# Fillers ahead of the weight and token tiles, and one common back transpose for a pair of heads

## The chip, the cores and the metric

The kernel runs on one core of a Trainium2 chip. The metric is the device time of one execution in microseconds (us). A core has five engines with a queue each: TensorE (PE in the rows; PEld is its loading of weights), VectorE (DVE), ScalarE (ACT), GpSimd (POOL) and SyncE (SP). They wait for each other by semaphores.

## The reference

Three layers follow each other; all numbers are float32, B = 4, S = 576, 8 heads of 64, model width 512.

```python
# 1 attention over the last row's maximum less tau
scores = q @ k.T / 8 ; scores = where(scores >= max - tau, scores, -1e9)
attn = exp(scores - max) ; attn /= sum(attn) + 1e-9 ; x = attn @ v
# 2 mixing along the sequence, then a feed-forward layer (512 -> 2048 -> 512)
u = x + (x.transpose(0, 2, 1) @ U @ V).transpose(0, 2, 1)
y = u + maximum(u @ w_ch1, 0) @ w_ch2
# 3 a causal gate of five taps, and two projections
gate = sigmoid(sum_k conv_w[k] * y shifted by 4 - k)
out = (gate * (y @ w_val)) @ w_out
```

The seven weights come as float64 and are turned into float32 by bit operations on the chip.

## The kernel before, in words

**Memory.** A tile takes a number of bytes in each of the 128 partitions of the on-chip memory (SBUF), and starts are rounded up to 32 bytes. Pools grow from the left end, or, with `side="right"`, from the right end. As the built program lays them out, every large tile on the left starts 96 bytes past a multiple of 256: `u`, `ring`, `w1_0`, `w2_0`, the staging tiles `raw`, `wt`, `wf`, the attention tiles `u4`, `vst`, `t_st`, `pt`, `pk`, `os`, `vt`, `vk`, `ns`, `e`, and later `y` and `w1_1`. Every tile on the right starts 224 bytes past one: `ld` (`qn`, `kn`, `tn`), `qk`, `st`, `bd`, and later `us`, `h` (and `g` in its place) and `w2_1`. The identity `idn` starts at 128. Steps inside the weight and token tiles are multiples of 512 bytes.

**Attention** (`attention`, from line 223) goes through 16 pairs of heads (`p`), each with 9 row tiles (`i`); one step of this is a slot `s = 9 p + i`. In a slot the code first issues the short work of the other engines and then PE's. `soft_max` (VectorE: negated scores and their minimum) comes first; then four phases 0 to 3 of functions put off by `later(slot, phase, fn, name)`, sorted within a phase by `LATE_ORDER`; `soft_exp` (ScalarE) follows phase 1 and `soft_mask` of the slot before (VectorE: mask and row sum) phase 2. Then PE gets the next slot's scores and the events that `put` gave this slot, sorted by `ORDER`: `prep_T` transposes q and k of the next pair (`tm`), `trans_main` and `trans_tail` transpose the masked exponentials (`xm`, `xk`; ScalarE copies them to `pt`, `pk`), `pv` multiplies by v (`o`, copied to `os`), `back` turns the result round again (`b`), and `mix_t`, `mix_u`, `mix_ut` add the mixing along the sequence (`t`, `u`, `ut`). All of these use one pool of four PSUM tiles. The order on every engine is this order of the code.

A pair's nine row tiles form three groups: group 0 is the 64 tail rows of both heads, groups 1 and 2 are 256 rows each. `pv` of groups 0 and 1 stands at slot offset 8, that of group 2 at 12; `back` of groups 0 and 1 at 10, that of group 2 at 14; `mix_t` at 15. Counted modulo 9, these are slots 8, 3, 1, 5 and 6. Each `back` takes one PSUM tile; in the slot after it VectorE multiplies by the reciprocal sums `r` into `ring` (L521), and for group 0 ScalarE does (`rb` L534, `ring` L536, twice). The first `back`'s VectorE and ScalarE instructions read the same PSUM tile, and VectorE's waits for ScalarE's. `soft_mask` makes the reciprocals in two parts, after row tiles 4 and 8 (L441, L442).

**Dense part.** `h1` multiplies 512 (last block 256) tokens of `us` by a chunk of `w_ch1` (`a`), `ch` multiplies `h` by a chunk of `w_ch2` (`c`): four chunks, five token blocks, taken alternately. `passes` (L771) does each in three products of high and low parts; a block is 4 x 12 = 48 matmuls. The weights of chunk c are in `w1_0`/`w2_0` for even c and in `w1_1`/`w2_1` for odd c. `val` (`v`, with `w1_0`) and `proj` (`p`, weights `g`, moving `w2_0`, L917) end the kernel; `val` waits for the gates, which VectorE sums up (L855). `dense_back` lays out `y` and `w1_1` where attention's tiles were.

Of the kernel before, what the change touches and what calls it, by code (L numbers as in the profile page):

```python
# [21 lines left out]
F32 = mybir.dt.float32  # L22
F32R = mybir.dt.float32r
I32 = mybir.dt.int32
U32 = mybir.dt.uint32
ACTF = mybir.ActivationFunctionType
ALU = mybir.AluOpType
# [9 lines left out]
def attention_moe_kernel(  # L37
# [15 lines left out]
    nc = tc.nc  # L53
    B, H, S, D = q.shape
# [8 lines left out]
    KD = DM // 128  # L63
    FC = 512
    NCH = DFF // FC
    SM = 512
    TL = S - SM
# [11 lines left out]
    const = ctx.enter_context(tc.tile_pool(name="const", bufs=1))  # L79
    idn = const.tile([128, 128], F32, name="idn")  # L80
# [4 lines left out]
    cw = const.tile([128, KC, KD], F32, name="cw")  # L85
    u = const.tile([128, KD, T], F32, name="u")
    ring = const.tile([128, 1280], F32, name="ring")
    w1_0 = const.tile([128, 2, KD, FC], F32R, name="w1_0")
    w2_0 = const.tile([128, 2, KD, FC], F32R, name="w2_0")
    wst_p = ctx.enter_context(tc.tile_pool(name="wst", bufs=2))  # L90
# [83 lines left out]
    class Staged:  # L174
# [20 lines left out]
    AT = {  # L195
        "pv": (8, 12), "t": 15, "ut": 18, "u": 18, "Tq": 0, "Tk": 1, "Tt": 2, "stA": 4, "bd": 4, "stB": 5,
        "lq": 1, "lv": 5,
    }
# [22 lines left out]
    low, top, mid, front, ps_x, ps_s, extra = (scope() for _ in range(7))  # L221

    def attention(dense_front, dense_mid, dense_back):
        setup = low.enter_context(tc.tile_pool(name="setup", bufs=1))
        sm_p = low.enter_context(tc.tile_pool(name="sm", bufs=4))
# [23 lines left out]
        st8 = [dict() for _ in range(NP)]  # L249

        def xtile(name):
            return x_ps.tile([128, 512], F32, tag="x", name=name)
# [47 lines left out]
        def later(s, k, fn, name=""):  # L300
            late[k].setdefault(s, []).append((LATE_ORDER.get(name, 0), fn))
# [126 lines left out]
        def row(p, i):  # L428
            return st8[p]["e", i][:, 1 - i % 2 if i else 0, :]

        def soft_mask(p, i):
            d = st8[p]
            e = row(p, i)
            nc.vector.scalar_tensor_tensor(  # L434
                out=e, in0=d.pop(("ns", i)), scalar=d.pop(("th", i))[:, 0:1], in1=e, op0=ALU.is_le, op1=ALU.mult,
                accum_out=d["sum"][:, i:i + 1],
            )
            if i in (4, 8):
                n = slice(0, 5) if i == 4 else slice(5, 9)
                t = d["sum"][:, n]  # L440
                nc.vector.tensor_scalar(out=t, in0=t, scalar1=1e-9, scalar2=None, op0=ALU.add)  # L441
                nc.vector.reciprocal(out=d["r"][:, n], in_=t)  # L442


        def trans_main(s, p, i):
# [41 lines left out]
        def pv(s, p, *gs):  # L487
            d = st8[p]
            ops = []
            for g in gs:  # L490
                n = 256 if g else TL
                pt = d.pop(("pt", g))
                o = xtile("o")
                nc.tensor.matmul(  # L494
                    o[:, 0:n], vk[p % 2].rearrange("p h d -> p (h d)"), d.pop(("pk", g)), start=True, stop=False
                )
                for j in range(4):
                    for hh in range(2):
                        rhs = pt[:, hh, j, :] if g else pt[:, j, hh * TL:(hh + 1) * TL]
                        ops.append((o[hh * D:(hh + 1) * D, 0:n], vt[p % 2][:, hh, j, :], rhs, j == 3))  # L500
                d["os", g] = os = o_p.tile([128, n], F32, tag=f"os{n}", name="os")
                later(s + 1, 0, lambda os=os, o=o, n=n: nc.scalar.activation(
                    out=os, in_=o[:, 0:n], func=ACTF.Copy), "o")
            for o, lhs, rhs, stop in ops:
                nc.tensor.matmul(o, lhs, rhs, start=False, stop=stop)  # L505


        def back(s, p, *gs):
            x = xtile("b")
            for g in gs:  # L510
                back_group(s, p, g, x)

        def back_group(s, p, g, x):
            d = st8[p]
            os, r = d.pop(("os", g)), d["r"]
            if g:
                for m in range(2):
                    nc.tensor.transpose(x[:, m * 128:(m + 1) * 128], os[:, m * 128:(m + 1) * 128], idn)

                def dve():  # L520
                    nc.vector.tensor_tensor(  # L521
                        out=x_of(p)[:, 2 * g - 2:2 * g, :].rearrange("p t (h d) -> p (t h) d", h=2),
                        in0=x[:, 0:256].rearrange("p (t d) -> p t d", t=4),
                        in1=r[:, 4 * g - 3:4 * g + 1].unsqueeze(2).to_broadcast([128, 4, D]), op=ALU.mult,
                    )

                later(s + 1, 2, dve, "n")
            else:
                x = x[0:TL, 256:384]
                nc.tensor.transpose(x, os[:, 0:TL], idn)  # L530
                rb = sm_p.tile([TL, 1], F32, tag="rb", name="rb")

                def act():
                    nc.scalar.activation(out=rb, in_=r[TL:128, 0:1], func=ACTF.Copy)  # L534
                    for hh, sc in ((0, r[0:TL, 0:1]), (1, rb)):
                        nc.scalar.activation(  # L536
                            out=x_of(p)[0:TL, 4, hh * D:(hh + 1) * D], in_=x[:, hh * D:(hh + 1) * D],
                            func=ACTF.Copy, scale=sc,
                        )

                later(s + 1, 1, act, "nt")

        def x_of(p):
            return ring[:, p % 2 * 640:(p % 2 + 1) * 640].rearrange("p (t d) -> p t d", t=5)
# [39 lines left out]
        for m in range(2):  # L584
# [7 lines left out]
            out=rv[0][:, 0:8 * R].rearrange("p (t r) -> p t r", t=4),  # L592
            in_=moe_U[0:SM, :].rearrange("(t p) r -> p t r", p=128),
# [3 lines left out]
        def load_V(a, o, c, n):  # L597
# [5 lines left out]
            out=qscale, in0=tau_sb, scalar1=0.0, scalar2=float(D) ** -0.5, op0=ALU.is_ge, op1=ALU.mult  # L603
# [39 lines left out]
        def put(s, what, *a):  # L643
            slots[s].append((what, a))

        for p in range(NP):
            s0 = 9 * p
            for i in range(9):
                put(s0 + i + 2, trans_main, p, i)
                if i % 2 == 0:  # L650
                    put(s0 + i + 2, trans_tail, p, i)
            put(s0 + AT["pv"][0], pv, p, 0, 1)
            put(s0 + AT["pv"][0] + 2, back, p, 0, 1)
            put(s0 + AT["pv"][1], pv, p, 2)
            put(s0 + AT["pv"][1] + 2, back, p, 2)
            if p + 1 < NP:
                s1 = s0
                put(s1 + AT["Tq"], prep_T, p + 1, "q")
                put(s1 + AT["Tk"], prep_T, p + 1, "k")
                put(s1 + AT["Tt"], prep_T, p + 1, "tail")  # L660
                put(s1 + AT["stA"], stacks, p + 1, 0)
                put(s1 + AT["bd"], tails, p + 1)
                put(s1 + AT["stB"], stacks, p + 1, 1)
            put(s0 + AT["t"], mix_t, p)
            put(s0 + AT["ut"] - (p == NP - 1), mix_ut, p)
            put(s0 + AT["u"] - (p == NP - 1), mix_u, p)
# [7 lines left out]
        for s in range(NS):  # L674
            p, i = divmod(s, 9)
# [12 lines left out]
            for m in (0, 1, 2, 3):  # L688
                for _, fn in sorted(late[m].pop(s, []), key=lambda x: x[0]):
                    fn()  # L690
                if m == 1 and live:
                    soft_exp(p, i)
                if m == 2 and 1 <= s <= 9 * NP:
                    soft_mask(*divmod(s - 1, 9))
                wtick(m)
# [21 lines left out]
        for _ in dense_front:  # L717
            work.tick()
        dense_back()
        ps_x.close()  # L720

# [3 lines left out]
    w1, w2 = [[w1_0], []], [[w2_0], []]  # L725
# [84 lines left out]
    def dense_back():  # L810
        extra.close()
        low.close()
        big = ctx.enter_context(tc.tile_pool(name="big", bufs=1))
        p1["y"] = big.tile([128, KD, B, YP], F32, name="y")
        w1[1].append(big.tile([128, 2, KD, FC], F32R, name="w1_1"))
        w2_p = ctx.enter_context(tc.tile_pool(name="w2", bufs=1, side="right"))
        w2[1].append(w2_p.tile([128, 2, KD, FC], F32R, name="w2_1"))
        nc.gpsimd.memset(p1["y"][:, :, :, 0:KC - 1], 0.0)
# [146 lines left out]
    with tc.manual_schedule():  # L965
        attention(dense_front(), dense_mid, dense_back)
        dense()
# [30 lines left out]
```

## Time and profile before

| | us |
|---|---|
| three runs | 869.0, 868.8, 867.21 (median 868.8) |
| profiled execution, its own time | 867.01 |
| its span, first to last instruction | 865.1 |
| PE busy | 834.6 (96%) |
| VectorE busy | 615.9 (71%) |
| ScalarE busy | 439.9 (51%) |
| GpSimd busy | 233.4 (27%) |

The share of busy time is a mean over stretches that differ, so the profile is read by stretch. A row of the chain of waits gives start, length and what PE or another engine did there; `x48` is the number of instructions joined in it. [...]

### The profile page before, as it was taken

How to read it: one execution, taken by the hardware profiler on the slowest of the kernel's cores; microseconds unless marked ns; L12 is line 12 of the kernel's file. 1: busy time of each engine (PE TensorE's matmuls, PEld its weight loads, DVE VectorE, ACT ScalarE, POOL GpSimd, SP SyncE). 2: the span in 40 equal slices, each digit the busy share in tenths (PEclk: the TensorE clock that was granted, in tenths of full speed). 3: DMA queues.
4: the chain of work that ended last, by engine and by line, in shares of the span. 5: the costliest groups of instructions: out<-in, count | busy, mean ns of one | idle time of the engine just before them, and what ended most of it. 6: DMA issues, size and time to landing. Idle time of an engine off the chain costs nothing.

```text
span 865.1 us, 14250 instructions
## 1 busy us (share of the span) xinstructions
PE 834.6 (96%) x5084; PEld 692.8 (80%) x5084; DVE 615.9 (71%) x1341; ACT 439.9 (51%) x890; POOL 233.4 (27%) x342
## 2 busy tenths in 40 slices
PE   8899999999999999899999999999999999999998
PEld 7687787788787887678888888888888888878886
DVE  5589889889989987436784685357753588988850
ACT  4487888888887887422333333133321334344532
POOL 6645422533322422001331243003420133200000
PEclk9799999999999999999999999999999999999999
DMA  5676755666676651001220122002110111001111
GB/s 129 147 151 124 172 125 125 153 154 137 151 168 135 132 113 44 0 1 49 73 74 25 48 74 74 1 1 84 62 50 1 41 57 49 1 1 49 49 49 74
DMA packets 63423, 68.07 MB, mean 79 GB/s; under 512 B 43333, under 2 KB 46549, under 8 KB 63354
## 3 DMA queue, kind: packets, MB, share of 16 engines
q1 hardware_dynamic: 61786, 64.07, 30.3%
q0 software_dynamic: 1424, 3.10, 1.3%
q8 instruction: 41, 0.67, 0.3%
q14 instruction: 28, 0.23, 0.1%
q10 hardware_dynamic: 144, 0.00, 0.0%
HBM read 35.89 MB, written 4.72 MB: 47 GB/s over the span
## 4 chain that ended last, share of the span: by engine, by line
PE 77%; DVE 9%; ACT 8%; issue 2%; SPq 1%; POOL 1%; DMA 1%; ACTq 0%; DVEq 0%; POOLq 0%
PE a L771 23%; PE c L771 20%; PE o L505 7%; PE s L395 6%; PE p L917 6%; PE xm L451 5%; PE v L771 5%; DVE u L855 3%; ACT e L423 2%; PE t L551 2%; PE o L494 2%; ACT pt L460 2%; DVE ns L409 1%; DVE e L434 1%; ACT qk L310 1%
## 5 line engine op out<-in xcount | busy, mean ns | idle before, releaser
L771 PE MATMUL a<-us,w 128*128 128x512 f32 (+1 forms) x960 | 205.6, 373 | 0.0
L771 PE MATMUL c<-h,w 128*128 128x512 f32 (+1 forms) x960 | 203.0, 370 | 1.3 <-ACT u L573 1.3
L771 PEld LDWEIGHTS a<-us,w 128*128 128x128 f32 x960 | 167.6, 188 | 33.9 <-issue 0.4
L771 PEld LDWEIGHTS c<-h,w 128*128 128x128 f32 x960 | 167.4, 188 | 33.7 <-ACT u L573 1.7
L779 ACT ACTIVATE h<-a 128x512 fp32r<-128x512 f32 (+1 forms) x80 | 44.2, 554 | 202.9 <-PE a L771 202.9
L780 DVE SCALAR_TENSOR_TENSOR h<-a,h 128x512 fp32r<-128x512 f32 (+1 forms) x80 | 51.0, 637 | 112.3 <-ACT h L779 112.2
L423 ACT ACTIVATE e<-ns,nm 128x576 f32<-128x576 f32 x144 | 111.5, 774 | 36.1 <-DVE ns L409 32.7
L128 POOL TENSOR_TENSOR wf<-wf,wt 128x512 f32<-128x512 f32 (+2 forms) x43 | 57.1, 1329 | 262.7 <-DVE wt L123 262.7
L424 POOL TENSOR_TENSOR th<-nm,tau_eff 128x1 f32<-128x1 f32 x144 | 72.8, 506 | 195.5 <-DVE ns L409 193.9
L434 DVE SCALAR_TENSOR_TENSOR e<-ns,th,e 128x576 f32<-128x576 f32 x144 | 119.8, 832 | 5.9 <-POOL th L424 5.5
L409 DVE TENSOR_SCALAR_CACHE_REDUCE ns<-s 128x576 f32<-128x576 f32 x144 | 107.8, 748 | 19.8 <-PE s L395 19.3
L451 PE MATMUL xm<-idn,e 128*128 128x128 f32 x576 | 88.5, 277 | 9.4 <-DVE e L434 5.1
L395 PE MATMUL s<-st 128*128 128x288 f32 x480 | 94.0, 317 | 1.3 <-DVE ns L409 1.1
L460 ACT ACTIVATE pt<-xm 128x512 f32<-128x512 f32 x144 | 84.5, 587 | 2.7 <-PE xm L451 0.6
L451 PEld LDWEIGHTS xm<-idn,e 128*128 128x128 f32 x576 | 69.1, 141 | 15.3 <-ACT pt L460 8.7
L395 PEld LDWEIGHTS s<-st 128*128 128x128 f32 x480 | 68.7, 191 | 13.5 <-DVE ns L409 6.6
L505 PE MATMUL o<-pt,vt 128*64 128x256 f32 (+1 forms) x768 | 70.9, 335 | 0.0
L505 PEld LDWEIGHTS o<-pt,vt 128*64 128x64 f32 x768 | 42.1, 140 | 25.2 <-issue 10.8
L169 POOL TENSOR_TENSOR w<-wf,w 128x512 fp32r<-128x512 f32 x36 | 54.2, 1518 | 10.3 <-ACT w L167 10.3
L832 DVE TENSOR_TENSOR y<-c,y 128x64 f32<-128x64 f32 (+4 forms) x96 | 39.9, 449 | 22.0 <-PE c L771 22.0
L855 DVE SCALAR_TENSOR_TENSOR u<-y,cw,u 128x576 f32<-128x576 f32 x64 | 55.0, 872 | 0.6
L756 DVE TENSOR_TENSOR us<-u,us 128x1024 fp32r<-128x1024 f32 (+1 forms) x40 | 46.8, 1211 | 9.2 <-ACT us L755 9.1
(108 smaller groups left out, 1043.8 us busy)
## 6 DMA issues: line engine op xcount, KB each, us to landing
raw<-in_moe_w_ch_dram SPq DMA_DIRECT2D x32, 512.0 KB, 4.1
st<-qk SPq DMA_DIRECT2D x30, 256.0 KB, 4.1
st<-qk SPq DMA_DIRECT2D x15, 432.0 KB, 4.0
st<-qk SPq DMA_DIRECT2D x45, 144.0 KB, 4.5
out_dram<-ring SPq DMA_DIRECT2D x18, 256.0 KB, 2.0
st<-qk SPq DMA_DIRECT2D x15, 288.0 KB, 4.9
qn<-in_q_dram SPq DMA_DIRECT2D x28, 128.0 KB, 3.8
kn<-in_k_dram SPq DMA_DIRECT2D x28, 128.0 KB, 3.6
```

The lines of the kernel that those rows point to most:

```text
L128: nc.gpsimd.tensor_tensor(out=dst, in0=dst, in1=tf, op=ALU.add)
L169: lo_eng.tensor_tensor(out=lo, in0=w, in1=f(hi), op=ALU.subtract)
L395: nc.tensor.matmul(s[:, n, 0:HS], lhs, rhs[:, n * HS:(n + 1) * HS], start=(m == 0), stop=(m == len(ops) - 1))
L409: nc.vector.tensor_scalar(out=ns.rearrange("p (a b) -> p a b", a=2), in0=s, scalar1=-1.0, scalar2=3.0e38, op0=ALU.mult, op1=ALU.min, accum ...
L423: nc.scalar.activation(out=row(p, i), in_=d["ns", i], func=ACTF.Exp, bias=nm[:, 0:1], scale=-1.0)
L424: nc.gpsimd.tensor_tensor(out=th, in0=nm, in1=tau_eff, op=ALU.add)
L434: nc.vector.scalar_tensor_tensor(out=e, in0=d.pop(("ns", i)), scalar=d.pop(("th", i))[:, 0:1], in1=e, op0=ALU.is_le, op1=ALU.mult, accum_o ...
L451: nc.tensor.transpose(x[:, j * 128:(j + 1) * 128], e[:, c + j * 128:c + (j + 1) * 128], idn)
L460: later(s + 1, 0, lambda: nc.scalar.activation(out=dst, in_=x.rearrange("p (j c) -> p j c", j=4), func=ACTF.Copy), "x")
L505: nc.tensor.matmul(o, lhs, rhs, start=False, stop=stop)
L771: nc.tensor.matmul(ps[:, 0:m1], lhs, rhs, start=(m == 0), stop=(m == len(ops) - 1))
L855: nc.vector.scalar_tensor_tensor(out=g, in0=y[:, e, b, k:k + S], scalar=cw[:, k, e:e + 1], in1=g, op0=ALU.mult, op1=ALU.add)
```

## The change

Two tiles that nothing uses are laid out: `pad_low`, 160 bytes, on the left behind `ring`, and `pad_top`, 224 bytes, as the first on the right. All tiles behind them move by as much, to starts that are multiples of 256; `u`, `ring` and `idn` stay. `w1_1` is laid out ahead of `y`, not behind it. `back` is called once a pair, at slot offset 14, for all three groups: the tail rows get a PSUM tile of their own (`x0`), groups 1 and 2 share one, and one VectorE instruction multiplies both. ScalarE's tail rows follow in phase 0 of the slot behind. The reciprocals are made in one part, after row tile 8. The copy of `o` to `os` is put off to phase 1 where it was phase 0.

```diff
+    const.tile([128, 40], F32, name="pad_low")
+    ctx.enter_context(tc.tile_pool(name="pad", bufs=1, side="right")).tile([128, 56], F32, name="pad_top")
     w1_0 = const.tile([128, 2, KD, FC], F32R, name="w1_0")
...
-            if i in (4, 8):
-                n = slice(0, 5) if i == 4 else slice(5, 9)
-                t = d["sum"][:, n]
+            if i == 8:
+                t = d["sum"]
                 nc.vector.tensor_scalar(out=t, in0=t, scalar1=1e-9, scalar2=None, op0=ALU.add)
-                nc.vector.reciprocal(out=d["r"][:, n], in_=t)
+                nc.vector.reciprocal(out=d["r"], in_=t)
...
-                later(s + 1, 0, lambda os=os, o=o, n=n: nc.scalar.activation(
+                later(s + 1, 1, lambda os=os, o=o, n=n: nc.scalar.activation(
...
+        def back(s, p):
             d = st8[p]
+            r = d["r"]
+            x0, x = xtile("b0"), xtile("b")
+            for g in (0, 1, 2):
+                os = d.pop(("os", g))
+                if not g:
+                    nc.tensor.transpose(x0[0:TL, 0:128], os[:, 0:TL], idn)
+                    continue
+                for m in range(2 * g - 2, 2 * g):
+                    nc.tensor.transpose(x[:, m * 128:(m + 1) * 128], os[:, m % 2 * 128:(m % 2 + 1) * 128], idn)
+            rb = sm_p.tile([TL, 1], F32, tag="rb", name="rb")
+
+            def act():
+                nc.scalar.activation(out=rb, in_=r[TL:128, 0:1], func=ACTF.Copy)
+                for hh, sc in ((0, r[0:TL, 0:1]), (1, rb)):
+                    nc.scalar.activation(
+                        out=x_of(p)[0:TL, 4, hh * D:(hh + 1) * D], in_=x0[0:TL, hh * D:(hh + 1) * D],
+                        func=ACTF.Copy, scale=sc,
+                    )
+            later(s + 1, 0, act, "nt")
+            later(s + 1, 2, lambda: nc.vector.tensor_tensor(
+                out=x_of(p)[:, 0:4, :].rearrange("p t (h d) -> p (t h) d", h=2),
+                in0=x.rearrange("p (t d) -> p t d", t=8),
+                in1=r[:, 1:9].unsqueeze(2).to_broadcast([128, 8, D]), op=ALU.mult,
+            ), "n")
...
             put(s0 + AT["pv"][0], pv, p, 0, 1)
-            put(s0 + AT["pv"][0] + 2, back, p, 0, 1)
             put(s0 + AT["pv"][1], pv, p, 2)
-            put(s0 + AT["pv"][1] + 2, back, p, 2)
+            put(s0 + AT["pv"][1] + 2, back, p)
...
+        w1[1].append(big.tile([128, 2, KD, FC], F32R, name="w1_1"))
         p1["y"] = big.tile([128, KD, B, YP], F32, name="y")
-        w1[1].append(big.tile([128, 2, KD, FC], F32R, name="w1_1"))
```

## Rows read from the trace of the kernel before

**Rows 1.** Stretch, us, busy us (count) of PE, PEld, DVE, ACT, POOL, PEclk, DMA
```profile
100.00:345.00 245.00, 233.89 (x1965) 195.15 (x1962) 213.09 (x594) 198.61 (x456) 82.89 (x164) 1.00 0.61 135
345.00:725.00 380.00, 375.95 (x1789) 311.03 (x1788) 227.31 (x385) 118.08 (x192) 86.50 (x62) 1.00 0.14 44
725.00:771.50 46.50, 44.81 (x241) 38.44 (x239) 43.09 (x70) 19.56 (x32) 6.62 (x4) 1.00 0.00 1
771.50:865.10 93.60, 89.63 (x407) 73.15 (x407) 55.59 (x84) 35.98 (x62) 0.00 (x0) 1.00 0.14 51
```

**Rows 2.** Chain of waits, dense part: start us, length us, what
```profile
563.15 5.74 PE c L771 x48
...
580.05 11.15 PE c L771 x48
591.20 11.15 PE a L771 x48
...
680.75 10.89 PE c L771 x48
691.64 11.16 PE a L771 x48
```

**Rows 3.** Chain of waits, from the end of the gates on
```profile
770.08 1.42 DVE us L756 x3
...
805.09 11.20 PE p L917 x48
```

**Rows 4.** Groups of instructions by form, 512-column matmuls: count | busy us, mean ns
```profile
L771 PE MATMUL a<-us,w 128*128 128x512 f32 x768 | 182.0, 395 | 0.0
L771 PE MATMUL c<-h,w 128*128 128x512 f32 x768 | 179.5, 392 | 1.3 <-ACT u L573 1.3
...
L917 PE MATMUL p<-w,g 128*128 128x512 f32 x216 | 50.9, 395 | 0.0
L771 PE MATMUL v<-us,w 128*128 128x512 f32 x192 | 45.7, 396 | 1.7 <-DVE us L756 1.1 <-ACT us L755 0.6
```

**Rows 5.** Chain of waits through one pair of the attention stage
```profile
167.29 0.20 ACT rb L534
...
167.51 0.51 ACT ring L536 x2
...
169.17 0.49 ACT pt L460
...
169.70 0.66 PE xm L451 x4
...
174.91 0.22 PE b L518 x2
...
176.21 1.13 PE t L551 x10
```

**Rows 6.** Chain of waits: the first and the last `rb` on it
```profile
43.94 0.20 ACT rb L534
...
329.95 0.20 ACT rb L534
```

**Rows 7.** Instructions in order of time, VectorE's multiplication in that pair
```profile
168.06 0.42 DVE L521 TENSOR_TENSOR ring<-b,r 128x256 f32<-128x256 f32 x1 [1.17 <-ACT ring L536]
```

**Rows 8.** Groups of instructions by form, VectorE: count | busy us, mean ns | idle before
```profile
L521 DVE TENSOR_TENSOR ring<-b,r 128x256 f32<-128x256 f32 x32 | 13.5, 421 | 7.9 <-ACT ring L536 7.8
...
L320 DVE TENSOR_TENSOR qk<-tm,qk 128x512 fp32r<-128x512 f32 x16 | 11.0, 685 | 0.0
...
L442 DVE RECIPROCAL r<-sum 128x5 f32<-128x5 f32 x16 | 3.0, 190 | 0.6
```

**Rows 9.** Chain of waits, the mix of the next pair
```profile
196.66 1.35 PE t L551 x10
```

**Rows 10.** Instructions in order of time, ScalarE ahead of that mix
```profile
195.99 0.59 ACT L460 ACTIVATE pt<-xm 128x512 f32<-128x512 f32 x1
```

**Rows 11.** Who waited for whom, GpSimd, 340 to 380 us: in total, times, longest
```profile
POOL y L818 <- PE ut L572: 31.9, 1, 31.9
```

More of the change, by code (lines that the diff above doesn't have):

```diff
@@ L505, in pv @@
                 nc.tensor.matmul(o, lhs, rhs, start=False, stop=stop)
[L508 to L513, printed above, removed]
-            d = st8[p]
[L515 to L524, printed above, removed]
-                    )
[L527 to L541, printed above, removed]
```

## The prediction

> **What bounds the kernel now.** I read the busy times by stretch first [rows 1], then the chain of waits inside each stretch [rows 2, 3, 5, 6 and 9], then single lines and their waits. [...] From 725 to 771.5 us VectorE is busy 43.09 of 46.5 us: the gates bind. In the attention stretch (100 to 345 us) PE is busy 234 of 245 us, with VectorE at 213 and ScalarE at 199: three engines near their limit, and the chain changes between them.
>
> **Part 1, the fillers.** They add no instruction. What they change is where a tile starts. Before, every large tile on the left of the memory starts 96 bytes past a multiple of 256 and every one on the right 224 bytes past one; after, those behind the fillers start at 0. So between a left and a right tile the distance is 128 modulo 256 before, and 0 after; between two tiles on one side it stays 0.
>
> The trace holds both cases. The blocks of 48 matmuls of 512 columns are alike in everything but their tiles. For `c` in chunks 1 and 3, moving `h` and weights `w2_1` are both on the right: a block takes 10.89 us (680.75 in [rows 2]). For `c` in chunk 2 the weights are `w2_0`, on the left: 11.15 us (580.05). `a` always has `us` on the right and `w1` on the left: 11.15 and 11.16 us. `p` has `g` on the right as weights and `w2_0` on the left as moving tile: 11.20 us [rows 3]. So I read the equal residue of the two tiles that PE reads together as worth 11.155 - 10.89 = 0.265 us a block, 5.5 ns a matmul. All five shown run at the same granted clock, and `c` and `a` alternate, so the load on the other engines does not sort them.
>
> The counts [rows 4], in blocks of 48: `a` 768/48 = 16, `c` 16, of which 8 (chunks 0 and 2) are slow, `v` 4, `p` 4.5. All of `a`, the slow `c` and `p` lie where the chain is PE. The first `v` block waits behind the gates (VectorE's 1.42 us of `us` ends before it [rows 3]), so what it gains is lost; 3 count. 16 + 8 + 3 + 4.5 = 31.5 blocks x 0.265 = **8.3 us less**. Blocks of 256 columns take 5.74 us with equal residues (563.15 in [rows 2], chunk 1); I take no change for them. Bounds of this term: nothing (the residue is not the cause), and on the other side that start addresses at 0 help more than equal residues do. From 256 to 512 columns a block grows by 10.89 - 5.74 = 5.15 us, so 512 columns cost 10.30 us a block by columns alone; 31.5 x (11.155 - 10.30) + 8 x (10.89 - 10.30) = 31.6 us less is the far end. I take 8.3 because it is the one that rows show, with no new kind of address.
>
> [...]
>
> In the attention stage operands mostly shift together and keep their distances. The identity, which lies ahead of the filler, does not; its distance to the transposed tiles changes from 32 or 160 to 128 (mod 256). Transposes take 0.11 us each (two in 0.22 us, [rows 5]); bounds: nothing, or the 5.5 ns above on each of 960 (60 a pair by the code), 5.3 us more. I take nothing: a transpose has a quarter of those columns.
>
> `w1_1` and `y` change places. `y` is a whole number of 256 bytes long, so this is not needed for the residue. The clearing of `y` now waits 31.9 us for the last mix of attention [rows 11]; that wait moves to earlier readers, and `w1_1`, whose writes come only after, takes over the wait for the mix. Cost 0, hidden by the dense blocks.
>
> **Part 2, the common back.** Per pair it removes one VectorE add and one reciprocal (0.19 us each by the reciprocal's row, so 0.38), and joins two multiplications of 256 elements (0.421 us each) to one of 512 (0.685 us by a VectorE row of that width) [rows 8]. It moves three transposes from slot 1 of the nine to slot 5, and the three ScalarE instructions of the tail rows (`rb`, `ring` twice) from slot 2 to slot 6.
>
> *What goes.* In 12 of 16 pairs these ScalarE instructions are on the chain: [rows 6] has the first and last. They run from 167.29 to 168.02 [rows 5], 0.73 us, and behind them come `qk`, `e`, and the `pt` copy (169.17) for which PE's next transposes wait until 169.70. Taken from there, `xm` starts 0.73 us earlier: 12 x 0.73 = 8.8 us less. VectorE's multiplication also waits there, 1.17 us, for ScalarE to finish with the same PSUM tile [rows 7]; with two tiles (`x0`, `x`) that wait goes, but it is off the chain in those pairs. What is late next is still ScalarE's row of copies and exponentials, so the whole 0.73 counts.
>
> *What comes back.* Slot 5 is on PE's path: `b`, two transposes, is on the chain at 174.91 [rows 5]. Three more at 0.11 us are 0.33 us; x 15 = 5.0 us more. In slot 6 the mix `t` now needs the whole product and the tail rows at once. In [rows 5] `t` takes 1.13 us, unhindered; in every second pair, where weight conversion delays ScalarE, 1.35 us [rows 9]. There the `pt` copy ends at 195.99 + 0.59 = 196.58 [rows 10]; the moved 0.73 us follow it, so `t` can start at 197.31 where it started at 196.66: 0.65 us, of which 0.33 is counted. 7 pairs x 0.32 = 2.2 us more. The longer multiplication ends 0.685 - 0.421 = 0.26 us later but starts 0.38 us earlier, since the add and reciprocal ahead of it are gone; in the 3 pairs where VectorE is the chain this gives 3 x 0.12 = 0.4 us less. Bounds per pair: nothing comes back, or all of it does, 0.33 + 0.73 + 0.26 = 1.32 us. Moving the `os` copy from phase 0 to 1 costs nothing: no other ScalarE work lies between.
>
> Attention: -8.8 + 5.0 + 2.2 - 0.4 = **2.0 us less**.
>
> **Sum.** 8.3 + 2.0 = 10.3 us off the profiled execution's 867.0: 856.7. The median of the runs shown is 1.8 us above that execution; I put half of this on top and predict 857.5.
>
> **Rivals.** *1. The fillers do nothing.* [...] Against: 10.89 us (once 10.93) in the six 512-column `c` blocks of chunks 1 and 3 that the chain shows, of which 680.75 is the fifth, and 11.1 to 11.2 elsewhere. Time: 867.0 - 2.0 + 0.9 = 866.
>
> *2. Starts at 0 free the rest too.* For: by column cost alone a block would take 10.30 us; 0.59 us remain even in the fast blocks, whose tiles start at 224. Against: nothing in the trace has such a start. Time: 867.0 - 31.6 - 2.0 + 0.9 = 834. [...]
>
> *3. The back costs nothing in slots 5 and 6*, because PE there catches up with VectorE anyway. For: VectorE is 87% busy in the stretch. Against: `b` and `t` are on the chain. Time: 867.0 - 8.3 - 9.2 + 0.9 = 850.
>
> *4. Slower: slot 6 becomes the stop.* `t` waits for the ScalarE rows, for the long multiplication and for the added transposes one after the other: 1.32 us x 15 = 19.8, less 8.8, is 11.0 us more; with the fillers' 8.3, 867.0 + 2.7 + 0.9 = 870.5. It decides from (8.8 + 8.3)/15 = 1.14 us a pair on. For: `t` already waits in every second pair. Against: ScalarE has its idle time in the slots just behind, and the tail rows are needed only by the last fifth of `t`, if its PSUM tile is free.
>
> **Chances.** Forecast 0.60, its own range 853 to 861; rival 1 0.15, rival 2 0.07, rival 3 0.10, rival 4 0.08. The range 847 to 866 holds the forecast, rival 3 and most of rival 1. Within 0.2% (1.7 us, about what can be told from no change) lies part of rival 1: same 0.06. Slower: rival 4 and a little, 0.09. Faster 0.85.
>
> **What would show it.** Right: `a`, `p` and all `c` blocks at 10.9 us; no ScalarE `rb` and `ring` between `pk` and `qk` on the chain; `t` at 1.1 to 1.4 us; VectorE's multiplication without its wait for ScalarE. Wrong: `a` blocks still at 11.15 (rival 1) or near 10.3 (rival 2); transposes above 0.11 us; `t` beyond 1.8 us in most pairs (rival 4).

## The result

The changed kernel takes 856.91 us (median of four runs, 854.32 to 859.88) against 868.15 us of the kernel before beside it: a ratio of 0.9879, 95% interval 0.9851 to 0.9907. Two later sets, beside other runs of the kernel before, gave 0.9874 (0.9857 to 0.9892) and 0.9873 (0.9849 to 0.9898). The prediction was 857.5. The profiled execution is one of the quickest: 854.32 us, span 852.4.

Busy times by stretch after the change, to lay beside [rows 1] (the stretches begin earlier, since what lies ahead of them is shorter):

```profile
100.00:345.00 245.00, 234.44 (x1958) 196.45 (x1957) 209.51 (x552) 198.57 (x457) 86.97 (x162) 1.00 0.56 130
345.00:714.30 369.30, 366.00 (x1767) 307.47 (x1766) 224.79 (x382) 114.38 (x185) 86.34 (x62) 1.00 0.14 45
714.30:761.00 46.70, 44.68 (x242) 38.54 (x241) 43.35 (x70) 19.69 (x32) 6.61 (x4) 1.00 0.00 1
761.00:852.40 91.40, 87.42 (x407) 73.03 (x407) 55.52 (x84) 35.96 (x62) 0.00 (x0) 1.00 0.14 52
```

The picture is the same: PE binds the dense part (busy for 366.00 of 369.3 us at a granted clock of 1.00), VectorE the gates (43.35 of 46.7 us), three engines the attention. What is shorter are the two dense stretches. The chain of waits there, and the end of it, against [rows 2 and 3]:

```profile
572.17 10.88 PE c L765 x48
583.05 10.88 PE a L765 x48
...
670.77 10.88 PE c L765 x48
...
771.92 10.88 PE p L911 x48
782.80 10.88 PE v L765 x48
...
826.32 5.75 PE v L765 x48
```

Blocks of 48 matmuls of 512 columns now take what only `c` with `w2_1` took before: 10.88 to 10.91 us wherever the chain shows one, but for the first `c` block (11.22; it was the longest before, too, with 11.43). A block of 256 columns stays at 5.75. The same matmuls by form, against [rows 4]:

```profile
L765 PE MATMUL a<-us,w 128*128 128x512 f32 x768 | 177.8, 390 | 0.0
L765 PE MATMUL c<-h,w 128*128 128x512 f32 x768 | 177.3, 390 | 1.3 <-ACT u L568 1.3
...
L911 PE MATMUL p<-w,g 128*128 128x512 f32 x216 | 49.6, 389 | 0.0
L765 PE MATMUL v<-us,w 128*128 128x512 f32 x192 | 44.6, 390 | 2.0 <-DVE us L750 1.1 <-ACT us L749 0.9
```

Records of single matmuls overlap (768 of 390 ns are 299.5 us, in 177.8 us busy), so the time of one is read from the length of a block over its count. Counts are equal, so the whole difference is the time of one matmul. The sums fall by 4.2, 2.2, 1.3 and 1.1 us, 8.8 in all; from the first `c` block on the kernel is 8.1 us shorter (below).

In attention, the chain through the pair that answers to [rows 5]:

```profile
163.28 0.17 ACT pk L484
163.45 0.50 ACT qk L315
...
163.97 0.70 DVE qk L323
...
164.71 0.66 PE xm L453 x4
...
169.97 0.11 PE b L517
170.07 0.44 PE b L520 x4
...
171.65 1.38 PE t L546 x10
```

No `rb` and `ring` stand between `pk` and `qk` any more; but `xm` now waits for VectorE's `qk` (line 323), which was not on the chain there. `b` is five transposes, `t` takes 1.38 us instead of 1.13.

**Where the 11 us come from.** Executions of one kernel differ in the first pair of attention (27.10 us in the profile above, 29.41 in that of the kernel before, 29.25 in the third set of the changed kernel) and in falls of the granted clock (below). So the parts are compared with the profile of the third set, span 854.4, whose first pair is like that before and whose clock stays at 1.00 behind the last mix and behind the gates. The marks are PE's first matmul of a stage in the traces; the 16 pairs are counted from the first `s` from `qk` alone to the start of the last pair's last scores.

| part | before, us | changed, us | difference | predicted |
|---|---|---|---|---|
| up to the first pair | 10.73 | 10.26 | -0.5 | |
| the 16 pairs | 328.66 | 326.60 | -2.1 | -2.0 |
| from there to the first `c` block | 39.35 | 39.29 | -0.1 | 0 |
| first `c` block to ScalarE's last `ring` | 483.11 | 475.04 | -8.1 | -8.3 |
| span | 865.1 | 854.4 | -10.7 | -10.3 |

The 0.5 us ahead of the first pair need not be the change's: this part takes 10.0 to 10.9 us over the profiles, 10.03 with the fillers alone and 10.89 with the back alone. The first pair's length goes with the place of a stretch at the lower clock. From 20 to 30 and from 30 to 40 us the granted clock is 0.94 and 0.55 in the kernel before (29.41 us), 0.90 and 0.59 in the third set (29.25), but 0.65 and 0.84 in the profile above (27.10).

### The profile page after: what moved, and what is told of

It reads as the page before. It is cut to its first block, busy times and chain, and to the rows that moved or that the text cites. A ratio compares the mean times of both kernels' runs of the same rounds, so it can differ in the third digit from the quotient of the medians.

```text
span 852.4 us, 14266 instructions
## 1 busy us (share of the span) xinstructions
PE 826.8 (97%) x5084; PEld 695.1 (82%) x5084; DVE 609.9 (72%) x1293; ACT 438.2 (51%) x890; POOL 241.5 (28%) x342
## 4 chain that ended last, share of the span: by engine, by line
PE 75%; DVE 10%; ACT 6%; issue 2%; DMA 2%; POOL 2%; SPq 1%; ACTq 0%; POOLq 0%; DVEq 0%
PE a L765 23%; PE c L765 20%; PE o L507 7%; PE p L911 6%; PE s L398 5%; PE v L765 5%; PE xm L453 4%; DVE u L849 3%; PE t L546 2%; PE o L496 2%; DVE e L437 1%; ACT pt L462 1%; DMA qn<-in_q_dram 1%; ACT e L426 1%; ACT qk L313 1%
## 5 line engine op out<-in xcount | busy, mean ns | idle before, releaser
L765 PE MATMUL c<-h,w 128*128 128x512 f32 (+1 forms) x960 | 200.9, 368 | 1.3 <-ACT u L568 1.3
L765 PE MATMUL a<-us,w 128*128 128x512 f32 (+1 forms) x960 | 201.5, 368 | 0.0
L427 POOL TENSOR_TENSOR th<-nm,tau_eff 128x1 f32<-128x1 f32 x144 | 81.5, 566 | 182.7 <-DVE ns L412 181.2
```

Source lines behind the costliest of these rows:

```text
L427: nc.gpsimd.tensor_tensor(out=th, in0=nm, in1=tau_eff, op=ALU.add)
L765: nc.tensor.matmul(ps[:, 0:m1], lhs, rhs, start=(m == 0), stop=(m == len(ops) - 1))
```

## Experiments

**1 and 2. The two halves of the change alone.** `e1_fillers` is the kernel before with the two filler tiles; `e2_back` is the changed kernel without them and with `y` and `w1_1` in their old order.

```diff
 e1_fillers, on the kernel before
+    const.tile([128, 40], F32, name="pad_low")
+    ctx.enter_context(tc.tile_pool(name="pad", bufs=1, side="right")).tile([128, 56], F32, name="pad_top")
     w1_0 = const.tile([128, 2, KD, FC], F32R, name="w1_0")
```

> The two fillers alone, on the kernel before; back, reciprocals and the order of y and w1_1 stay as before. Theory: equal residues speed up the dense blocks and do nothing else: all 512-column blocks of a, c, v and p at 10.88 to 10.89 us, the attention stage as long as before, the time 8.3 us below the kernel before. Rival (the fillers also change the attention stage, where the changed kernel came out 4.7 us shorter up to its first c block): 10 us or more below before, with the first c block well ahead of 378.7 us.

> The common back and the single reciprocal alone; no fillers, y and w1_1 in the old order. Theory: what leaves slots 1 to 3 comes back in slots 5 and 6: slot lengths on PE as in the changed kernel (slot 1 near 1.52 us, slot 3 near 4.2, slot 5 near 1.6, slot 6 near 2.6), dense blocks as before (a 11.15 us), the time 0 to 2 us below before. Rival (the common back gives all that the dense blocks do not): 4 to 5 us below before, with the first c block near 374 us.

`e1_fillers`: 859.35 us, ratio 0.9894 (0.9877 to 0.9911). `e2_back`: 867.86 us, ratio 1.000 (0.9985 to 1.0014). The chain of waits with the fillers alone, dense part:

```profile
586.89 10.88 PE a L773 x48
```

The fillers alone bring the blocks to 10.88 us and most of the gain; the slots of attention keep their lengths within 0.03 us. So the placing of the tiles is the cause of the dense gain. With the back alone the slots come out as expected (1.52, 4.15, 1.59 and 2.62 us for slots 1, 3, 5 and 6), and the time measures as nothing, though in its profile the 16 pairs are 2.6 us shorter (326.02 against 328.66): what takes that away in this profile is found below, under 7.

**3 and 4. Which placing it is.** `e3_equal224` has a single filler of 128 bytes on the left, so that all large tiles start at 224 modulo 256. `e4_distances` leaves `us`, `h` and `g` at 224 and puts each weight tile at another distance.

```diff
 e3_equal224, on the kernel before
+    const.tile([128, 32], F32, name="pad_low")
     w1_0 = const.tile([128, 2, KD, FC], F32R, name="w1_0")
 e4_distances, on the kernel before
+    const.tile([128, 8], F32, name="pad_a")
     w1_0 = const.tile([128, 2, KD, FC], F32R, name="w1_0")
+    const.tile([128, 8], F32, name="pad_b")
     w2_0 = const.tile([128, 2, KD, FC], F32R, name="w2_0")
...
+        big.tile([128, 8], F32, name="pad_c")
         w1[1].append(big.tile([128, 2, KD, FC], F32R, name="w1_1"))
...
         w2[1].append(w2_p.tile([128, 2, KD, FC], F32R, name="w2_1"))
+        w2_p.tile([128, 40], F32, name="pad_d")
```

> The kernel before with one filler of 128 bytes on the left and none on the right: every large tile, left or right, starts 224 bytes past a multiple of 256. Theory (only the distance of the two tiles that PE reads counts): all 512-column blocks 10.88 to 10.89 us, as with the fillers, and about 8 us below before. Rival (the starts themselves must be multiples of 64 or 256): a and p stay at 11.15 us and more, time as before.

> The kernel before with small fillers that set each weight tile apart; us, h and g stay at 224. Distance of moving tile to weights modulo 256: a in even chunks 96, c in even chunks 64, a in odd chunks 32, c in odd chunks 160, p 192. Theory (any distance but 0 costs the same): all blocks 11.1 to 11.2 us, c in odd chunks now too, time about 1.6 us above before. Rival 1 (multiples of 64 are enough): c in even chunks and p at 10.89, the rest slower. Rival 2 (the cost grows with the distance, up to 128): a odd fastest, a even slowest of these.

`e3_equal224`: 860.38 us (one run), its blocks as fast as with starts at 0 (one of `c`):

```profile
576.66 10.88 PE c L772 x48
```

So a start at a multiple of 256 is not needed; what the fast cases share is the distance 0 between the two tiles. Equal starts were run at 0 and at 224 only, so a rule by each tile's own start that favours just these two is not ruled out. `e4_distances`: 868.1 us (one run), about the time of the kernel before where I expected 1.6 us more. Its chain of waits shows one distance a line: `a` in even chunks 96, `c` in even chunks 64, `a` in odd chunks 32, `c` in odd chunks 160, `p` 192:

```profile
412.56 11.20 PE a L773 x48
423.75 10.99 PE c L773 x48
...
513.21 11.20 PE a L773 x48
524.41 11.24 PE c L773 x48
...
806.00 11.20 PE p L921 x48
```

My expectation, that every distance but 0 costs the same, missed one: at 64 a block costs 0.11 us more than at 0, at the other four 0.31 to 0.36. Neither rival's list fits either. The distance is counted from the weights to the moving tile, and the direction matters: `w2_0` lies 64 away from `h` and from `g` alike, and costs 0.11 us as weights (`c`) but 0.32 as the moving tile (`p`, 192).

**5. With its own weights, or with the next?** PE loads the next weights while a matmul runs (in the changed kernel's trace matmuls start at 599.89, 600.12 and 600.35 us, and with each a weight load of 0.19 us; in the 380 us from 345 on in [rows 1], PE is busy for 376 and PEld for 311), so the moving tile could collide with either. `e8_which_load` is `e1_fillers` with the low halves (index 1) of `us` and `w1_0` shifted by 128 bytes: in even chunks two of three products then have moving data and their own weights at unequal residues, in odd chunks one of three.

```diff
 e8_which_load, on e1_fillers
+    def shifted(t):
+        return t[:, :, 0:KD * FC].rearrange("p a (k f) -> p a k f", k=KD)
...
-    w1_0 = const.tile([128, 2, KD, FC], F32R, name="w1_0")
+    w1_0 = shifted(const.tile([128, 2, KD * FC + 32], F32R, name="w1_0"))
...
-        t = (pool or p1["us"]).tile([128, 2, KD, NB], F32R, tag="us", name="us")
+        t = shifted((pool or p1["us"]).tile([128, 2, KD * NB + 32], F32R, tag="us", name="us"))
```

> The fillers alone, and in us and w1_0 the low parts lie 128 bytes further on (mod 256) than the high parts. In a of even chunks the three products of a step are high x high, high weights x low tokens, low weights x high tokens: the distance of a moving tile to its own weights is 0, 128, 128, that to the weights of the next matmul, which are loaded meanwhile, is 0, 0, 0. In a of odd chunks (w1_1 unshifted) own and next distances are 0, 128, 0. Theory (what collides is the moving tile's reading with the loading of the next weights): a even 10.88 us, a odd 10.97 us. Rival (the distance to its own weights counts): a even 11.06, a odd 10.97. Second rival (the low halves' own start counts, not a distance): a even 11.06, too, and a odd 10.97 with the slow ones being other matmuls.

858.85 us (one run). Chain of waits, an even and an odd chunk:

```profile
409.80 11.08 PE a L776 x48
420.88 10.90 PE c L776 x48
...
448.33 10.99 PE a L776 x48
```

My theory (the next weights, 10.88 in even chunks) fell; the rival (its own weights, 11.06 and 10.97) gives 11.08 and 10.99. The second rival (the low halves' own start) gives the same block times and, worked out, the same slow product in odd chunks, where only the low half of `us` is shifted; so it is not separated here. In odd chunks the single matmuls agree too: by the starts of PE's records only the shifted product is slow (234 ns from start to start, the others 226 to 227). In even chunks all three lie at 229 to 233 ns instead of one at 227 and two at 234. So the size of the effect is known and its mechanism inside PE is not.

**6. Two edits beside it.** `e7_y_first` is the changed kernel with `y` ahead of `w1_1` again; `e6_mix_later` is the changed kernel with the mix `t` one slot later, away from the tail rows for which it waits.

```diff
 e6_mix_later, on the changed kernel
-"t": 15
+"t": 16
```

> The changed kernel with y laid out ahead of w1_1 again, both still at multiples of 256. Theory (the swap costs and brings nothing): dense blocks at 10.88 us, time as the changed kernel within its spread of 5 us, no new wait ahead of the first c block. Rival (the clearing of y waits for the last mix and holds up the weights behind it): a wait of PE for weights in the first dense blocks, 1 us or more.

> The changed kernel with the mix t one slot later (offset 16, slot 7 of the nine). Theory (in slot 6 PE waits for ScalarE's tail rows, which hold the mix's PSUM tile and operand, 0.2 to 0.3 us a pair): the wait goes, slots 6 and 7 together fall from 3.59 to 3.3 us, 3 to 4 us less than the changed kernel, ratio 0.985. Rival (the attention stage then stops at ScalarE or VectorE in the next pair's slots 0 to 3): slots 6 and 7 shorten and slots 8 to 3 take it back; time as the changed kernel.

`e7_y_first`: 856.68 us (one run), blocks 10.88, and from the first `c` block to the last `ring` 475.04 us as in the third set of the changed kernel: the exchange of places does nothing. `e6_mix_later`: 862.13 us (861.98 to 862.29), ratio 0.9939 (0.9926 to 0.9952), 5.7 us above the changed kernel beside it (856.39, run 7). Chain of waits, the pair's slots 6 to 8, where VectorE's `t_st` now comes late:

```profile
178.04 0.16 ACT t_st L547
...
179.35 0.29 DVE t_st L548
```

and who waits for it (waiter, what it waits for: total us, times, longest):

```profile
PEld o L496 <- DVE t_st L548: 6.3, 11, 1.0
```

Slot 6 falls from 2.61 to 1.14 us as hoped (`t` is out of it), slot 7 takes 1.44 of that back, and slot 8 grows by 0.49, because `pv`'s `o` now waits for `t_st`. My theory fell. The rival had the place (slot 8) right, but not the price: it expected no change of time. One slot later is no way round what the back costs in slot 6.

**7. The changed kernel again.** The four runs of the first set stand far apart, so the kernel was run again.

> The changed kernel once more, with more runs beside the kernel before. Theory: the back gives next to nothing, so its time is that of the fillers alone, 0.989 of before within 0.002. Rival (back and fillers together give more than each alone, as the first runs' 856.9 us hinted): 0.985 to 0.987.

856.39 us (854.64 to 859.6), ratio 0.9874 (0.9857 to 0.9892). The interval holds values of the theory (0.987 to 0.991) and of the rival (0.985 to 0.987), and it overlaps with that of the fillers alone (0.9877 to 0.9911): by the times it stays open whether the back adds anything to the fillers. Taken with the first set and the third, 16 runs: eleven from 853.88 to 857.12, at a mean granted clock of 0.990 to 0.994, and five from 859.15 to 859.88, all at 0.988. The profiled run of the third set is of the first kind, that of the second set (859.6) of the second. Busy times around the last mix (columns as in [rows 1]), first of the third set; PE is idle for two of the four us to 366:

```profile
362.00:366.00 4.00, 1.99 (x14) 1.59 (x13) 1.29 (x2) 1.31 (x4) 0.00 (x0) 1.00 0.01 4
366.00:370.00 4.00, 4.00 (x19) 3.29 (x19) 0.82 (x2) 0.77 (x2) 0.00 (x0) 1.00 0.00 0
```

The same stretch in the second set, and one behind the gates:

```profile
362.00:366.00 4.00, 1.99 (x14) 1.61 (x13) 1.29 (x2) 1.31 (x4) 0.00 (x0) 0.95 0.01 4
366.00:370.00 4.00, 4.00 (x13) 3.15 (x12) 0.00 (x0) 0.00 (x0) 0.00 (x0) 0.62 0.00 0
...
765.00:775.00 10.00, 10.00 (x39) 8.06 (x38) 9.17 (x16) 3.34 (x5) 0.00 (x0) 0.83 0.00 0
```

PE does the same up to the end of `t` (365.7 us). Then the granted clock is 0.62 on the mean (0.50 is the lowest level in the profiles of the kernel before, from 30 to 38 us, and of the changed kernel, from 24 to 32 us), and 13 matmuls are done against 19. Its chain of waits:

```profile
363.56 0.69 DVE ring L532
...
364.30 1.38 PE t L546 x10
365.68 7.05 PE a L765 x24
```

The 24 matmuls of `a` take 7.05 us instead of 5.46 in the third set: 1.6 us lost. A second fall stands behind the gates' last stall (765 to 775 us, 0.83); that one is in the profile of `e1_fillers` as well (0.83), so it is not the back's. Both together are about the 3 us between the two kinds of run. The profile of `e2_back` has both falls: 7.12 us for the same 24 matmuls, and 0.85 behind the gates; in this profile that accounts for its 2.6 us. Of its twelve runs four lie from 864.6 to 866.0 (mean clock 0.989 to 0.992) and eight from 867.5 to 869.8 (0.985 to 0.988). Not all of the spread is from there: the kernel before, with no such fall in its profile, reaches from 864.6 to 869.5 us beside these runs.

**8. Is it the gap ahead of the last mix?** In the kernel before PE also waits there, but less (1.7 us ahead of `t`, against 2.0), and `t` itself waits less. Chain of waits, before:

```profile
366.81 0.42 DVE ring L521
...
367.27 0.94 PE t L551 x6
368.21 5.58 PE a L771 x24
```

The longer multiplication (0.69 against 0.42 us) and the 1.38 us of `t` make the weak stretch some 0.7 us longer. `e9_last_split` and `e11_last_split_again` are one kernel, in which the last pair alone keeps the split back and its two reciprocals; `e10_after_third` is the changed kernel beside it; `e12_gap_filled` leaves the common back and puts idle transposes into the gap.

```diff
 e9_last_split, on the changed kernel (split_back is the old back)
-            put(s0 + AT["pv"][1] + 2, back, p)
+            if p == NP - 1:
+                put(s0 + AT["pv"][0] + 2, split_back, p, 0, 1)
+                put(s0 + AT["pv"][1] + 2, split_back, p, 2)
+            else:
+                put(s0 + AT["pv"][1] + 2, back, p)
 e12_gap_filled, on the changed kernel, first lines of mix_t
+            if p == NP - 1:
+                warm(14)
```

> The changed kernel, but the last of the 16 pairs keeps the split back of the kernel before: its rows come in two parts with two reciprocals. Theory: with the common back, PE stands still for about 2 us ahead of the last mix t (360.29 to 362.29 in the changed kernel's profile), then t waits inside itself (1.38 us against 0.94), and in part of the executions the granted clock falls behind this gap (profiles of the common back alone and of the second run of the changed kernel: 0.59 and 0.62 for the 4 us from 366, the 24 matmuls of a behind t 7.1 us instead of 5.5). With the split back in the last pair t takes 0.94 us again, the clock stays at 1.00 there, the transition to the first c block is at most 39.4 us in each profile, and the time is steady, 854 to 856.5, median 855.3, about 1 us below the changed kernel. Rival: the gap of about 1.7 us that the kernel before has in the same place is as good a cause, or the clock falls whatever stands there; then the executions still spread from 854.5 to 859.5 and the median stays at 856.4.

> The changed kernel itself, unaltered, beside the version with the last pair's split back. Both theories: 856.4 median; single executions near 854.6, 856.3 and 859.4, those near 859 with a granted clock below 1 behind the last mix t.

> The version with the last pair's split back a second time. If the gap ahead of the last mix is what lets the granted clock fall, none of its executions stands near 859.4 again and all lie from 854.5 to 857; in 16 executions of the changed kernel five stood from 859.1 to 859.9, at a mean clock of 0.988. If the five executions of the first time were luck, about one in three stands near 859.

> The changed kernel, with 14 transposes of the identity, whose result nothing reads, in PE's order between the 12 matmuls of a and the last mix t: 14 x 0.11 = 1.5 us in the 2 us in which PE stands still there, so they cost nothing themselves. Theory (the gap is what lets the clock fall): the granted clock stays at 1.00 behind t, t starts no later, no execution stands near 859.4, median 855.5 to 856.3. Rival (the clock falls for another reason, such as the work of the whole stretch): executions near 859.4 at a mean clock of 0.988 are there as before, about one in three, and the median stays at 856.4 or a little above.

| kernel | median, us | from, to | ratio to before, 95% | runs above 859 |
|---|---|---|---|---|
| changed, 2nd and 3rd set | 856.39, 856.65 | 853.88, 859.85 | 0.9873 (0.9849 to 0.9898), 3rd | 3 of 12 |
| last pair split, 1st | 855.72 | 854.98, 856.97 | 0.9869 (0.9847 to 0.9892) | 0 of 5 |
| last pair split, 2nd | 856.11 | 854.72, 856.81 | 0.9867 (0.9847 to 0.9888) | 0 of 6 |
| gap filled | 856.35 | 854.26, 856.45 | 0.9868 (0.9847 to 0.9888) | 0 of 5 |

With the last pair split (`e9_last_split`), `t` and what follows are as short as in the kernel before, and the way to the first `c` block takes 38.93 us (38.91 the second time):

```profile
363.43 0.94 PE t L586 x6
364.36 5.47 PE a L809 x24
```

With the gap filled, the same stretch (busy times, PE 3.52 of 4 us instead of 1.99) and the chain:

```profile
362.00:366.00 4.00, 3.52 (x29) 3.15 (x28) 1.29 (x2) 1.31 (x4) 0.00 (x0) 1.00 0.01 4
366.00:370.00 4.00, 4.00 (x19) 3.32 (x18) 0.99 (x2) 0.77 (x2) 0.00 (x0) 1.00 0.00 0
```

```profile
364.06 1.38 PE t L548 x10
365.44 5.47 PE a L767 x24
```

Five of 16 runs of the changed kernel stand above 859, and none of the 16 with the gap shortened or filled; if the share were the same, so lopsided a split would come up in 2 of 100 cases (4368 of 201376 ways to choose five of 32). That is less firm than it looks: the bound of 859 was drawn after the first runs were seen, and only one set of the changed kernel (1 of 6) stands beside one of the others (0 of 5). Among the profiles, a fall behind the last mix is in two of the five with the common back and `t` in its place, and in none of the eight with the split back or the filled gap there. So the gap is the likely cause of the runs above 859, and not shown to be. In the median these versions are not told apart from the changed kernel: all intervals overlap, and the 1 us that I expected of the split does not show. What they seem to do is take the runs near 859 away.

## Why the prediction was right

**Fillers, 8.3 us predicted, 8.1 measured.** The 8.3 us were for 31.5 blocks, of which two lie ahead of the part where 8.1 were measured; the others were priced at 7.8. The reason held: equal residue modulo 256 of the two tiles that PE reads together. `e1_fillers` and `e3_equal224` show it, with starts at 0 and at 224 alike (10.88 us a block). 10.89 us, read from one kind of block in the old trace, is what all kinds take now. Rival 1 (the fillers do nothing, 866) is ruled out by `e1_fillers`, rival 2 (starts at 0 free the rest, 10.30 us a block) by 10.88 in every block. Starts at multiples of 32 bytes, which every run had, gave blocks of 512 columns of 10.88 to 11.24 us (without the first `c` block).

**Common back, 2.0 us predicted, 2.1 measured between two profiles.** That the two agree to 0.1 us is luck: the terms are off by more than that, one wait was not seen, and by the times the back's share is not clear of noise (0.9985 to 1.0014 alone). Lengths of the nine slots of a pair, means of pairs 2 to 14, from PE's records:

| slot | 0 | 1 | 2 | 3 | 4 | 5 | 6 | 7 | 8 |
|---|---|---|---|---|---|---|---|---|---|
| before | 2.326 | 2.258 | 1.654 | 3.984 | 1.099 | 1.314 | 2.373 | 0.972 | 4.533 |
| changed | 2.308 | 1.522 | 1.648 | 4.177 | 1.106 | 1.587 | 2.614 | 0.971 | 4.519 |

- What goes: predicted 0.73 us in 12 pairs, 8.8, as ScalarE's `rb` and `ring` ahead of `xm`. On PE it is slot 1 that is 0.74 us shorter on the mean, for other reasons: 0.33 are the three transposes that left it, 0.36 a wait of `tm`. Before, `tm` waited behind `b` in slots 1 and 2 until VectorE had read a PSUM tile of the common pool, which I had not seen. Two rows of who waited for whom, before (total us, times, longest):

```profile
PEld tm L335 <- DVE ring L521: 6.9, 14, 0.8
...
PEld tm L332 <- DVE qk L316: 5.9, 13, 0.5
```

  After, `tm` waits for VectorE nowhere. How much of the gain is owed to this, and how much to ScalarE's rows, no run separates. "What is late next is still ScalarE's row" was the step that failed: it is VectorE's low part of `qk`, in front of slot 3's `xm`, which gives 0.19 back. That leaves 0.55 a pair, 8.2 us in 15 pairs: less a pair than I said, in more of them. Two rows of the same kind, after:

```profile
PE xm L453 <- DVE qk L323: 6.0, 13, 0.5
...
PEld t L546 <- ACT ring L526: 4.9, 13, 0.7
```

- `b` in slot 5: predicted 0.33 a pair, measured 0.27.
- `t` in slot 6: predicted 0.32 in every second pair. It waits for the tail rows in most pairs (second line above: PE's load waits 13 times for `ring`): 0.24 a pair on the mean, 3.6 in 15 pairs instead of 2.2 - 0.4. The chain where it bites, 0.81 us from the end of `pt` to `t` as [rows 9 and 10] had led me to expect (0.73 and an issue):

```profile
190.68 0.48 ACT pt L462
...
191.18 0.20 ACT rb L524
...
191.41 0.52 ACT ring L526 x2
...
191.97 1.38 PE t L546 x10
```

- VectorE's multiplication no longer waits for ScalarE, against the 1.17 us of [rows 7], and takes the predicted 0.69 us (group by form):

```profile
L532 DVE TENSOR_TENSOR ring<-b,r 128x512 f32<-128x512 f32 x16 | 11.0, 686 | 0.0
```

Rival 3 (slots 5 and 6 cost nothing) and rival 4 (1.14 us a pair or more) are both out: the two slots give back 0.51 us a pair, 7.7 in 15. With hundredths in the other slots, pairs 2 to 14 end up 0.06 us shorter each, 0.8 in all (single ones from 0.56 shorter to 0.67 longer). Another 0.8 is in the last pair, whose slot 3 alone is 1.1 us shorter, and 0.5 in the first two.

**The cover that I costed at nothing.** The clearing of `y` still waits for the last mix, 32.6 us as against 31.9 in [rows 11]: the wait did not move to earlier readers, as I had said it would. It is hidden all the same, and the exchange of places costs nothing (`e7_y_first`). Transposes stay at 0.11 us.

**What it left out.** My sum has no term of its own for the last mix and the way into the dense part. In three of the five profiles with the common back there none is needed (39.29 against 39.35 us); in the other two a fall of the clock worth 1.6 us follows the longer gap ahead of the last mix. This may be why the back alone measured as 1.000 and not as 0.998, and why single runs of the changed kernel stand near 859; the profiles fit, but do not prove it.

## What to carry to other kernels

Look whether blocks that differ only in their operands' places take different times, and read the placing off the fast ones: the pace of 512-column matmuls went with the distance, modulo 256 bytes, between the moving tile and its weights (10.88 us a block of 48 at 0, 10.99 to 11.24 at the six others measured), and one 128-byte filler tile was enough. Sum a reordering slot by slot, with what each slot gives back; here 7.7 of 8.2 us came back in two other slots. Ask of each instruction that leaves a slot which tile of a shared pool it held, and who waited for it. Look at the granted clock behind a stall: here it fell behind one of 2 us in two of five profiles with the common back (0.59 and 0.62 over 4 us; in the second, 7.05 us for 24 matmuls instead of 5.46), and 14 idle transposes in the gap cost nothing (856.35 us against 856.39 and 856.65).

## What was not expected of the hardware

- The price by distance is no step at zero. A block of 48 matmuls of 512 columns took 10.88 to 10.91 us (once 10.93) at distance 0, 10.99 to 11.00 at 64, 11.19 to 11.21 at 32 and at 96, 11.14 to 11.20 at 128, 11.20 at 192, 11.24 at 160: 0.11 to 0.36 us, or 2 to 7.5 ns a matmul (the first `c` block, 0.3 us longer in every run, is left out). Blocks of 256 columns took 5.74 to 5.76 us at distance 0 and 5.65 to 5.77 at the others: there equal residues gained nothing.
- The granted clock fell for some us behind a stall of 2 us in one execution of the changed kernel (0.62 over the 4 us from 366) and not in another (1.00), with the engines' work the same up to there. What decides it was not found.
- The first pair of attention takes from 27.1 to 29.4 us in the three profiles compared. The mean granted clock from 20 to 40 us is the same in all three (0.745); where in it the clock is low differs, and the length with it.
